# Attention's loads in another order on the load queue, with one-word stores between them that wait for computed tiles

## The chip, the cores and the metric

The kernel runs on one core of a Trainium2 chip. A core has a matrix engine (TensorE, PE in the profile; PEld are its weight loads), a vector engine (VectorE, DVE), a scalar engine (ScalarE, ACT), GpSimd (POOL) and SyncE (SP), which in this kernel issues every load and store. Each engine runs its own instructions in order and waits on semaphores for the others. Sixteen DMA engines move data between HBM and the core's memory. The metric is the device time of one execution in microseconds: 512.07 is the median of three runs before the change (509.72 to 512.94).

## The reference

Three layers in float32, one behind the other. First attention with 4 batches, 8 heads, 512 local and 32 global tokens of 64 features: local tokens attend to a window of 32 positions on either side and to the global tokens, global tokens attend to all. Then a gated MLP, then a soft mixture of experts.

```python
k_all = np.concatenate([k_g, k_l], axis=2)
v_all = np.concatenate([v_g, v_l], axis=2)
out_g = np.matmul(sm(scale * np.matmul(q_g, k_all.transpose(0, 1, 3, 2))), v_all)
s_ll = scale * np.matmul(q_l, k_l.transpose(0, 1, 3, 2))
s_ll = np.where(np.abs(pos[:, None] - pos[None, :]) <= 32, s_ll, -1000000000.0)
s_lg = scale * np.matmul(q_l, k_g.transpose(0, 1, 3, 2))
out_l = np.matmul(sm(np.concatenate([s_lg, s_ll], axis=-1)), v_all)
...
x = (silu(x @ w_gate) * (x @ w_val)) @ w_out      # 2304 tokens, 512 -> 1536 -> 512
...
logits = x @ phi                                  # then 8 experts with 4 slots each
```

## The kernel before

Attention comes first and takes about the first 110 us of the span. It is cut into 8 steps n, each a batch with half of its heads, and each step into two halves tp; the 16 halves are the units u = 2n + tp. For every unit TensorE computes scores (`stage_scores`, L346), VectorE adds the mask and finds the largest (L357), ScalarE takes exponentials (`stage_exp`, L367), TensorE transposes them (`stage_pT`, L376), ScalarE copies the transposes into two tiles pT (L379), and TensorE multiplies them with the values (`stage_pv`, L390). This is a software pipeline: in the loop's pass u stand the scores and exponentials of unit u, the transposes and values of unit u - 1 and the last transposes (`stage_xT`) of unit u - 2. The global tokens of step n have their scores in its even unit (`stage_gscores`, L451; exponentials into pG, L466 to L473), and their values in the next step's even unit (`stage_gpv`, L499).

The loads of a step are queries qT (512 KB, `load_q`, L204), keys kS (736 KB, `load_k`, L208) and values (960 KB in five loads, `load_v`, L228 to L236). Each has two buffers by turns, so that a load of step n + 2 (for values: n + 1) waits until the work of the step that held the buffer has read it. GpSimd copies values into two shifted layouts (`turn_v`, L242 to L247) and spreads queries into the form that the scores need (`spread_q`, L264). A load waits also for the one that stands eight places ahead of it in the order of issue, since eight semaphores go around.

MLP's matrices come as 64-bit words that a helper turns into float32 in five steps p0 to p4 (`w_prep`): `w_load` brings a tile raw of 512 KB; p0 takes its absolute values on ScalarE (L136) and shifts on VectorE (L137); p2 issues the load of the tile two further on. In attention one such step runs in each unit (`prep_some`), right behind the unit's scores and ahead of the copies into pT. Steps are there from the end of unit 4 on, so that p0 of raw0 stands in unit 5 and p0 of raw1 in unit 10.

All loads stand in one queue of SyncE, in the order of the code. An instruction there that waits holds up all behind it. In the loop before, the calls stand in this order:

```python
load_k(n + 2)            # odd units, behind the exponentials
...
load_q(n + 2); load_v(n + 1)      # even units, at the end
...
if u == 2: w_load(0); w_load(1); # and phi
```

Of the kernel before, what the change touches and what calls it, by code (L numbers as in the profile page):

```python
# [8 lines left out]
F32 = mybir.dt.float32  # L9
# [11 lines left out]
P = 128  # L21
# [4 lines left out]
NQ = B * 2  # L26
# [10 lines left out]
def window(i):  # L37

    if i == 0:
        return 0, "A", 0  # L40
    m, k = divmod(i - 1, 3)
    return (4 * m, 4 * m + 2, 4 * m + 3)[k], "ABC"[k], m
# [3 lines left out]
def attention_moe_soft_moe_kernel(  # L46
# [15 lines left out]
    nc = tc.nc  # L62
# [19 lines left out]
    dram = ctx.enter_context(tc.tile_pool(name="dram", bufs=1, space=bass.MemoryType.DRAM))  # L82
# [6 lines left out]
    phi_sb = cpool.tile([P, NC, NS], F32, name="phi_sb")  # L89
# [4 lines left out]
    for i, (_, n) in enumerate(BLOCKS):  # L94
        pool = x2pool if i in GROUPS[-1] else x1pool
        t = pool.tile([P, 2 * NC * n * P], F32R, name=f"x{i}")
        t = t.rearrange("p (a c n) -> p a c n", a=2, c=NC)
# [9 lines left out]
    def ring_tile(i, name, dt=F32R):  # L107
        p = rings[0] if i % 3 == 0 else rings[1]
        return p.tile([P, 4, DM], dt, name=name, tag=f"w{i % 3}")

    def w_load(q):
        if q >= 3 * NFC:
            return
        c, k = divmod(q, 3)
        fs = slice(c * P, c * P + P)
        t = wraws[q] = wtmp.tile([P, NC * P, 2], U32, tag="raw", name=f"raw{q}", bufs=2)
        if k < 2:
            nc.sync.dma_start(
                t.rearrange("p (c f) w -> p c (f w)", c=NC),
                (w_gate, w_val)[k][:, fs].rearrange("(c p) f -> p c f", p=P).bitcast(U32),  # L120
            )
        else:
            nc.sync.dma_start(t.rearrange("p f w -> p (f w)"), w_out[fs, :].bitcast(U32))
# [3 lines left out]
    def w_prep(q):  # L127

        c, k = divmod(q, 3)
        d = {}  # L130

        def p0():
            raw = d["raw"] = wraws.pop(q)
            d["t"] = wtmp.tile([P, NC * P], U32, tag="wbits", name=f"wb{q}", bufs=3)
            d["v"] = wtmp.tile([P, NC * P], F32, tag="wabs", name=f"wv{q}")
            nc.scalar.activation(d["v"], raw[:, :, 1].bitcast(F32), AF.Abs)  # L136
            nc.vector.tensor_scalar(  # L137
                out=d["t"], in0=raw[:, :, 1], scalar1=3, scalar2=0x3FFFFFFF,
                op0=ALU.logical_shift_left, op1=ALU.bitwise_and,
            )  # L140

        def p1():
            nc.vector.scalar_tensor_tensor(  # L143
                out=d["t"], in0=d["raw"][:, :, 0], scalar=29, in1=d["t"],
                op0=ALU.logical_shift_right, op1=ALU.bitwise_or,
            )

        def p2():
            nc.vector.scalar_tensor_tensor(  # L149
                out=d["t"], in0=d["raw"][:, :, 1], scalar=0xC0000000, in1=d["t"],  # L150
                op0=ALU.bitwise_and, op1=ALU.bitwise_or,
            )
            w_load(q + 2)

        def p3():
            w = d["t"].bitcast(F32)
            nc.vector.scalar_tensor_tensor(  # L157
                out=w, in0=d["v"], scalar=F64_NORMAL, in1=w, op0=ALU.is_ge, op1=ALU.mult
            )
            if k == 0:  # L160
                wchunk[c] = ring_tile(c, f"w{c}")
                wkept[c] = dram.tile([P, 4, DM], F32, name=f"w_d{c}")

        def p4():
            w = d["t"].bitcast(F32)
            if k == 2:
                wo[c] = w
                nc.sync.dma_start(wo_d[:, c], w)
                return
            wh, wl = wchunk[c][:, 2 * k], wchunk[c][:, 2 * k + 1]  # L170
            nc.scalar.activation(wh, w, AF.Copy)  # L171
            nc.gpsimd.tensor_tensor(out=wl, in0=w, in1=wh, op=ALU.subtract)  # L172
            ks = slice(2 * k, 2 * k + 2)
            nc.sync.dma_start(wkept[c][:, ks], wchunk[c][:, ks].bitcast(F32))

        prep.extend((p0, p1, p2, p3, p4))

    def prep_some(n=1):
        for _ in range(min(n, len(prep))):
            prep.pop(0)()  # L180
# [21 lines left out]
    def load_q(n):  # L202
        qT[n] = aqk.tile([P, 2, S], F32, tag="qT", name=f"qT{n}")
        nc.sync.dma_start(qT[n], qT_d[n])  # L204

    def load_k(n):
        kS[n] = aqk.tile([P, 2, KBLK * 32], F32, tag="kS", name=f"kS{n}")
        nc.sync.dma_start(kS[n], kS_d[n])  # L208
# [45 lines left out]
    def spread_q(n, a, eng, xs=slice(0, 16)):  # L254

        rows = slice(64 * a, 64 * a + 64)
        dst = qB[n % 2][rows].rearrange("p (a x g) -> p a x g", a=2, g=64)[
            :, :, xs, 32 * a : 32 * a + 32
        ]
        src = qT[n][rows].rearrange("p a (x q) -> p a x q", q=32)[:, :, xs]  # L260
        if eng is nc.scalar:
            nc.scalar.activation(dst, src, AF.Copy)
        else:
            eng.tensor_copy(dst, src)  # L264
# [28 lines left out]
    for g in (0, 1, 3, 2):  # L293
# [7 lines left out]
        for r in range(3):  # L301
            first = next(i for i in range(1, 16) if i % 3 == r and i % 2 == bl)
            p0 = first // 2
            n = len(range(p0, 8, 3))
            k = window(first)[1]
# [24 lines left out]
    st = {}  # L330
# [32 lines left out]
    def stage_exp(u):  # L363
        d = st[u]
        for hp in range(2):
            for bp in range(4):
                nc.scalar.activation(  # L367
                    d["p"][hp][:, bp], d["sm"][hp][:, bp], AF.Exp,
                    bias=d["nm"][:, hp, bp : bp + 1], scale=-1.0, accum_out=d["rs"][:, bp, hp : hp + 1],
                )  # L370

    def stage_pT(u, hp):
        d = st[u]
        pt = ps_tr.tile([P, 4, P], F32, tag="tr", name=f"ppT{u}_{hp}")
        for bp in range(4):
            nc.tensor.transpose(pt[:, bp], d["p"][hp][:, bp], ident)  # L376
        pT = awk.tile([P, 4, P], F32, tag=f"pT{hp}", name=f"pT{u}_{hp}")
        d["pT", hp] = pT
        nc.scalar.activation(pT, pt, AF.Copy)  # L379
# [34 lines left out]
    def split_rest():  # L414
        while rest:
            rest.pop(0)()
# [99 lines left out]

    mstack = ExitStack()
    NU = len(units)
    load_k(1)
    for u in range(NU):  # L520
        n, tp = units[u]
        stage_scores(u)
        split_rest()
        prep_some()
        if u >= 1:
            stage_pT(u - 1, 0)
            stage_pT(u - 1, 1)
        stage_exp(u)
        if tp == 1 and n + 2 < NQ:
            load_k(n + 2)  # L530
        if u == 0:

            turn_v(0, 0, 3)
        if tp == 0 and n + 1 < NQ:
            spread_q(n + 1, 0, nc.gpsimd)
        if u == 0:
            turn_v(0, 3, 5)
        if tp == 0 and n + 1 < NQ:
            if n > 0:
                spread_q(n + 1, 1, nc.gpsimd)  # L540
        if u == 1:
            spread_q(1, 1, nc.vector)
        if tp == 0:
            stage_gscores(n)
            stage_gexp(n)
        else:
            stage_gpT(n, 0)
        if u >= 1:
            stage_pv(u - 1)
        if tp == 1:  # L550
            stage_gpT(n, 3)
        if u >= 1 and tp == 0:
            stage_gpv(n - 1)
        if tp == 1 and n + 1 < NQ:
            turn_v(n + 1)
        if u >= 2:
            stage_xT(u - 2)
        if tp == 0 and n + 2 < NQ:
            load_q(n + 2)
        if tp == 0 and n + 1 < NQ:  # L560
            load_v(n + 1)
        if u == 2:
            w_load(0)
            w_load(1)
            nc.sync.dma_start(phi_sb, phi.rearrange("(c p) s -> p c s", p=P))
        if u == 4:
            for q in range(3):
                w_prep(q)
    for a in range(4):
        rows = slice(32 * a, 32 * a + 32)  # L570
        nc.gpsimd.tensor_copy(istack[rows], ident[rows, rows])
# [236 lines left out]
    gate(0, 0, G1[0], False)  # L808
    stage_pT(NU - 1, 0)
    stage_pT(NU - 1, 1)  # L810
    stage_xT(NU - 2)
    stage_gpv(NQ - 1)
    split_rest()
    stage_pv(NU - 1)
    prep_some(len(prep))
    gate(0, 0, G1[1], False)
    stage_xT(NU - 1)
    split_rest()
# [36 lines left out]
    for c in range(NFC):  # L855
# [6 lines left out]
        k = S1 * c + 13 if last else S1 * (c + 1) + 3  # L862
# [61 lines left out]
    t = epool[0].tile([P, 4096], F32, name="dr0", tag="e0")  # L924
    t = [t[:, 512 * k : 512 * k + 512] for k in range(5)]
# [17 lines left out]
    k = base + 30  # L943
# [148 lines left out]
    t = dpool.tile([P, 4 * NF], F32, tag="Ts", name="sT")  # L1092
    nc.gpsimd.memset(t[:, : 5 * E * DG], 0.0)  # L1093
    t = t[:, : 5 * E * DG].rearrange("p (c k) -> p c k", c=5)
# [69 lines left out]
    for k in range(3, 2 * E):  # L1164
# [4 lines left out]
        if side == 0:  # L1169
            t = epool[slot > 0].tile([P, 4096], F32, name=f"f{slot}", tag=f"e{slot}")  # L1170
# [22 lines left out]
    for i in range(5, NEARLY):  # L1193
        t = epool[1].tile([P, 4096], F32, name=f"ob{i}", tag=f"e{i}")
# [141 lines left out]
```

## Time and profile before

| | before |
|---|---|
| median of the runs | 512.07 us (509.72 to 512.94) |
| the profiled execution | 514.79 us, span 513.0 us |
| TensorE busy | 482.3 us, 94% |
| VectorE, ScalarE, GpSimd busy | 306.9, 181.4, 127.9 us |
| bytes moved by DMA | 107.63 MB |

The span runs from the first instruction of the program to its last in the profiled execution; starts below are counted from its beginning. TensorE's busy share is high everywhere but in the first twentieth. [...] A piece called issue in the chain of waits is time in which an engine waited for nothing that the profile shows.

### The profile page before, as it was taken

To read this page: it belongs to the slowest core of one execution; us is meant where nothing else is said; L and a number is where in the kernel's file an instruction comes from. 1 tells how busy PE (TensorE), PEld (TensorE's weight loads), DVE (VectorE), ACT (ScalarE), POOL (GpSimd) and SP (SyncE) were. 2 spreads that over 40 slices of the span, in tenths; PEclk is the share of its full clock that TensorE was granted. 3 is DMA by queue.
4 is the path that set the end of the run, shared out by engine and by line. 5 is a ranking of instruction groups with operands and counts; after the bars stand their busy time and mean duration, and the time that the engine had idled before them with its cause. 6 is when DMAs were issued, how large, how long until landed. Compare 5 with 4: busy or idle time off the path is not lost.

```text
span 513.0 us, 12537 instructions
## 1 busy us (share of the span) xinstructions
PE 482.3 (94%) x5092; PEld 379.7 (74%) x5092; DVE 306.9 (60%) x801; ACT 181.4 (35%) x542; POOL 127.9 (25%) x199
## 2 busy tenths in 40 slices
PE   6698999999999999999999999999999999889972
PEld 4587788788778788778777877787799988532741
DVE  7667888777976786777776677353233434452022
ACT  5868898892233222222223321121111012310021
POOL 7886798630322222112112221000000000010000
PEclk8999999999999999999999999999999999999997
DMA  8987585412744554444445473133099996699996
GB/s 216 298 224 230 172 262 148 120 44 63 227 167 149 166 181 145 161 160 165 143 145 169 152 248 135 56 118 132 6 380 391 411 414 212 241 423 419 357 349 193
DMA packets 50433, 107.63 MB, mean 210 GB/s; under 512 B 3464, under 2 KB 35016, under 8 KB 47176
## 3 DMA queue, kind: packets, MB, share of 16 engines
q1 hardware_dynamic: 50376, 106.84, 61.5%
q8 instruction: 40, 0.66, 0.5%
q14 instruction: 17, 0.14, 0.1%
HBM read 86.64 MB, written 20.19 MB: 208 GB/s over the span
## 4 chain that ended last, share of the span: by engine, by line
PE 80%; ACT 5%; DVE 5%; DMA 5%; issue 2%; SPq 2%; ACTq 0%; DVEq 0%
PE pval L602 28%; PE pgate L602 28%; PE sc L346 4%; PE psh L1132 3%; PE T L768 3%; PE o L390 2%; ACT p L367 2%; DMA f<-in_w_dram 2%; PE ppT L376 2%; DMA wo<-wo_d 2%; PE L L677 2%; SPq L900 2%; PE pwp L648 2%; DVE sm L357 1%; PE pwt L638 1%
## 5 line engine op out<-in xcount | busy, mean ns | idle before, releaser
L602 PE MATMUL pgate<-x,w 128*128 128x512 f32 x432 | 108.8, 396 | 0.0
L602 PE MATMUL pval<-x,w 128*128 128x512 f32 x432 | 107.1, 396 | 0.0
L602 PEld LDWEIGHTS pval<-x,w 128*128 128x128 f32 x432 | 80.2, 188 | 20.0 <-issue 2.2
L602 PEld LDWEIGHTS pgate<-x,w 128*128 128x128 f32 x432 | 80.2, 188 | 17.6
L617 DVE SCALAR_TENSOR_TENSOR u<-u,pgate 128x512 f32<-128x512 f32 (+2 forms) x60 | 36.5, 608 | 77.4 <-ACT u L616 76.2
L616 ACT ACTIVATE u<-pgate 128x512 f32<-128x512 f32 (+2 forms) x60 | 31.8, 530 | 126.9 <-PE pgate L602 68.3
L172 POOL TENSOR_TENSOR w<-wb,w 128x512 fp32r<-128x512 f32 x24 | 31.4, 1308 | 110.6 <-ACT w L171 62.6
L626 DVE SCALAR_TENSOR_TENSOR u<-u,pval 128x512 f32<-128x512 f32 (+2 forms) x60 | 36.3, 605 | 35.7 <-PE pval L602 35.7
L367 ACT ACTIVATE p<-sm,nm 128x128 f32<-128x128 f32 x128 | 49.4, 393 | 0.0
L602 PE MATMUL pval<-x,wr 128*128 128x384 f32 (+1 forms) x288 | 47.8, 312 | 0.0
L171 ACT ACTIVATE w<-wb 128x512 fp32r<-128x512 f32 x24 | 15.2, 632 | 92.1 <-DVE wb L157 49.4
L602 PE MATMUL pgate<-x,wr 128*128 128x384 f32 (+1 forms) x288 | 47.7, 311 | 0.0
L602 PEld LDWEIGHTS pval<-x,wr 128*128 128x128 f32 x288 | 43.3, 188 | 5.1 <-issue 5.1
L602 PEld LDWEIGHTS pgate<-x,wr 128*128 128x128 f32 x288 | 43.5, 188 | 3.8 <-issue 3.7
L346 PE MATMUL sc<-kS,qB 128*64 128x128 f32 x512 | 34.2, 282 | 6.0 <-ACT pG L470 3.0
L346 PEld LDWEIGHTS sc<-kS,qB 128*64 128x64 f32 x512 | 28.7, 139 | 11.1 <-issue 6.2
L357 DVE CUSTOM_DVE_ANT_0 sm<-sc,masks 128x128 f32<-128x128 f32 x128 | 28.6, 287 | 6.4 <-PE sc L346 4.6
L1093 POOL MEMSET sT<- 128x1440 f32 x1 | 1.3, 1297 | 123.7 <-PE U L1068 123.7
L157 DVE SCALAR_TENSOR_TENSOR wb<-wv,wb 128x512 f32<-128x512 f32 x36 | 24.9, 692 | 3.8 <-DVE wb L149 0.5
L660 POOL COPY wp<-ws 32x32 f32<-32x32 f32 x48 | 11.8, 246 | 60.2 <-DVE ws L653 58.7
L629 DVE STREAM_TRANSPOSE hT<-u 128x512 f32<-128x512 f32 x36 | 25.6, 712 | 1.3
L143 DVE SCALAR_TENSOR_TENSOR wb<-raw,wb 128x512 uint32<-128x512 uint32 x36 | 25.0, 693 | 1.1
(209 smaller groups left out, 728.6 us busy)
## 6 DMA issues: line engine op xcount, KB each, us to landing
e<-in_w_dram SPq DMA_DIRECT2D x7, 2048.0 KB, 13.1
w_d<-w SPq DMA_DIRECT2D x24, 512.0 KB, 2.6
wr<-w_d SPq DMA_DIRECT2D x12, 1024.0 KB, 7.1
f<-in_w_dram SPq DMA_DIRECT2D x10, 1024.0 KB, 12.8
raw<-in_wgate_dram SPq DMA_DIRECT2D x12, 512.0 KB, 3.6
raw<-in_wval_dram SPq DMA_DIRECT2D x12, 512.0 KB, 4.0
raw<-in_wout_dram SPq DMA_DIRECT2D x12, 512.0 KB, 3.6
kS<-in_kS_dram SPq DMA_DIRECT2D x7, 736.0 KB, 7.0
```

Source lines behind the costliest of these rows:

```text
L143: nc.vector.scalar_tensor_tensor(out=d["t"], in0=d["raw"][:, :, 0], scalar=29, in1=d["t"], op0=ALU.logical_shift_right, op1=ALU.bitwise_or,)
L157: nc.vector.scalar_tensor_tensor(out=w, in0=d["v"], scalar=F64_NORMAL, in1=w, op0=ALU.is_ge, op1=ALU.mult)
L172: nc.gpsimd.tensor_tensor(out=wl, in0=w, in1=wh, op=ALU.subtract)
L346: nc.tensor.matmul(sc[64 * (i % 2) : 64 * (i % 2) + 64, i // 2], qb[:, hp, blk], kS[n][:, hp, 32 * s0 : 32 * s0 + 128], start=True, stop=T ...
L357: nc.vector.tensor_tensor_reduce(out=sm[:, bp], in0=sc[:, bp], in1=masks[:, 4 * tp + bp], scale=-SCALE, scalar=3e38, op0=ALU.add, op1=ALU.min,
L367: nc.scalar.activation(d["p"][hp][:, bp], d["sm"][hp][:, bp], AF.Exp, bias=d["nm"][:, hp, bp : bp + 1], scale=-1.0, accum_out=d["rs"][:, b ...
L602: nc.tensor.matmul(ps[:, :n], w[:, 2 * k + a, cc * P : cc * P + P], xt[b][:, cc], start=(cc == 0 and i == 0), stop=(cc == NC - 1 and i == 2),)
L616: nc.scalar.activation(u[:, :n], pg[:, :n], AF.Tanh, scale=0.5)
L617: nc.vector.scalar_tensor_tensor(out=u[:, :n], in0=u[:, :n], scalar=1.0, in1=pg[:, :n], op0=ALU.add, op1=ALU.mult)
L626: nc.vector.scalar_tensor_tensor(out=u[:, :n], in0=u[:, :n], scalar=0.5, in1=pv[:, :n], op0=ALU.mult, op1=ALU.mult)
L629: nc.vector.transpose(out=hT[blk][:, c], in_=u[:, :n])
L768: nc.tensor.matmul(d["T"][i][32 * gg : 32 * gg + 32, 0:NF], rs[bi][r, 32 * j : 32 * j + 32], hT[blks[bi]][r, :, 32 * j : 32 * j + 32], sta ...
```

## The change

Only calls that issue loads are put elsewhere, and five stores are added. `pace(k, t)` stores one element of a tile t into a small DRAM tile; its place in SyncE's queue makes the queue wait until t is computed. Keys and queries of step 2 stand in unit 1 behind such a store of pT of unit 0, so that the values of step 1 are ahead of them. Queries of step 3 stand in unit 3. Queries of step n + 2 for n from 2 to 5 stand early in unit 2n, behind a store of pT of unit 2n - 1. The loads raw0, raw1 and phi move from unit 2 to units 4, 6 and 7. What the steps of `w_prep` do, and where, is as before.

```diff
--- before.py
+++ after.py
@@ -516,6 +516,12 @@
 
     mstack = ExitStack()
     NU = len(units)
+    paced = dram.tile([1, 16], F32, name="paced")
+
+    def pace(k, t):
+
+        nc.sync.dma_start(paced[:, k : k + 1], t)
+
     load_k(1)
     for u in range(NU):
         n, tp = units[u]
@@ -525,8 +531,17 @@
         if u >= 1:
             stage_pT(u - 1, 0)
             stage_pT(u - 1, 1)
+        if u == 1:
+            pace(0, st[0]["pT", 0][0:1, 0, 0:1])
+            load_k(2)
+            load_q(2)
+        if tp == 0 and n > 1 and n + 2 < NQ:
+            pace(n, st[u - 1]["pT", 0][0:1, 0, 0:1])
+            load_q(n + 2)
         stage_exp(u)
-        if tp == 1 and n + 2 < NQ:
+        if tp == 1 and 0 < n and n + 2 < NQ:
+            if n == 1:
+                load_q(3)
             load_k(n + 2)
         if u == 0:
 
@@ -535,9 +550,8 @@
             spread_q(n + 1, 0, nc.gpsimd)
         if u == 0:
             turn_v(0, 3, 5)
-        if tp == 0 and n + 1 < NQ:
-            if n > 0:
-                spread_q(n + 1, 1, nc.gpsimd)
+        if tp == 0 and n + 1 < NQ and n > 0:
+            spread_q(n + 1, 1, nc.gpsimd)
         if u == 1:
             spread_q(1, 1, nc.vector)
         if tp == 0:
@@ -555,17 +569,16 @@
             turn_v(n + 1)
         if u >= 2:
             stage_xT(u - 2)
-        if tp == 0 and n + 2 < NQ:
-            load_q(n + 2)
         if tp == 0 and n + 1 < NQ:
             load_v(n + 1)
-        if u == 2:
+        if u == 4:
             w_load(0)
-            w_load(1)
-            nc.sync.dma_start(phi_sb, phi.rearrange("(c p) s -> p c s", p=P))
-        if u == 4:
             for q in range(3):
                 w_prep(q)
+        if u == 6:
+            w_load(1)
+        if u == 7:
+            nc.sync.dma_start(phi_sb, phi.rearrange("(c p) s -> p c s", p=P))
     for a in range(4):
         rows = slice(32 * a, 32 * a + 32)
         nc.gpsimd.tensor_copy(istack[rows], ident[rows, rows])
```

The first place is SyncE's queue in units 0 to 2 (vA, vB, vC are the values' layouts, the number behind a name is the step or the buffer). Before:

```order
L208 DMA kS1_198<-in_kS_dram 128x1472
L204 DMA qT2_267<-in_qT_dram 128x1024
L228 DMA vA1_117<-in_vl_dram 96x5x256
L229 DMA vA1_117<-in_vg_dram 32x5x256
L233 DMA vB1_118<-in_vl_dram 32x256
L235 DMA vC1_119<-in_vl_dram 64x4x256
L236 DMA vC1_119<-in_vl_dram 32x256
L208 DMA kS2_328<-in_kS_dram 128x1472
L204 DMA qT3_535<-in_qT_dram 128x1024
```

And with the change:

```order
L208 DMA kS1_199<-in_kS_dram 128x1472
L228 DMA vA1_117<-in_vl_dram 96x5x256
L229 DMA vA1_117<-in_vg_dram 32x5x256
L233 DMA vB1_118<-in_vl_dram 32x256
L235 DMA vC1_119<-in_vl_dram 64x4x256
L236 DMA vC1_119<-in_vl_dram 32x256
L523 DMA paced_198<-pT0_0_310 1x1
L208 DMA kS2_320<-in_kS_dram 128x1472
L204 DMA qT2_322<-in_qT_dram 128x1024
```

The five loads of the second values moved up two places past the third queries, and a store stands between them and the third keys.

The second place is the same queue in units 2 to 4, from the last load of the third values on. Before:

```order
L236 DMA vC0_116<-in_vl_dram 32x256
L118 DMA raw0_542<-in_wgate_dram 128x4x256
L118 DMA raw1_544<-in_wval_dram 128x4x256
L565 DMA phi_sb_81<-in_phi_dram 128x4x32
L208 DMA kS3_602<-in_kS_dram 128x1472
L204 DMA qT4_815<-in_qT_dram 128x1024
L228 DMA vA1_117<-in_vl_dram 96x5x256
```

With the change, from the queries of step 3 on:

```order
L204 DMA qT3_597<-in_qT_dram 128x1024
L208 DMA kS3_599<-in_kS_dram 128x1472
L523 DMA paced_198<-pT3_0_699 1x1
L204 DMA qT4_709<-in_qT_dram 128x1024
L228 DMA vA1_117<-in_vl_dram 96x5x256
L229 DMA vA1_117<-in_vg_dram 32x5x256
L233 DMA vB1_118<-in_vl_dram 32x256
L235 DMA vC1_119<-in_vl_dram 64x4x256
L236 DMA vC1_119<-in_vl_dram 32x256
L118 DMA raw0_820<-in_wgate_dram 128x4x256
L208 DMA kS4_881<-in_kS_dram 128x1472
```

raw0 stood right behind the third values; it now stands behind the five loads of the fourth values, and raw1 and phi are further back. The keys of step 3 are no longer behind them.

The third place is ScalarE in units 4 and 5 with the change, with the semaphores that each instruction waits for; the rows are the same before but for numbers.

```order
L473 ACTIVATE pG_112,grs2_733<-gt2_722,gm2_729 128x32 [waits PE_49,Activation_49]
L409 ACTIVATE x0_82<-pxT2_809 128x2x256 [waits PE_49]
L136 ACTIVATE wv0_856<-raw0_820 128x512 [waits DMAHW3_49]
L379 ACTIVATE pT4_0_864<-ppT4_0_859 128x512 [waits PE_49,Activation_49]
L379 ACTIVATE pT4_1_871<-ppT4_1_866 128x512 [waits PE_49,Activation_49]
L367 ACTIVATE p5_0_822,rs5_824<-sm5_0_826,nm5_825 128x128 [waits DVE_49,Activation_49]
```

Nothing moved on ScalarE: the first work on raw0 stands ahead of the copies into pT4 and the exponentials p5. The orders of TensorE, VectorE and GpSimd are the same as well.

## Rows read from the trace of the kernel before

**Rows 1.** The page's part 1: engine, busy us, share of the span, instructions.
```profile
PE 482.3 (94%) x5092; PEld 379.7 (74%) x5092; DVE 306.9 (60%) x801; ACT 181.4 (35%) x542; POOL 127.9 (25%) x199
```

**Rows 2.** Chain of waits in order of time, first 160 us: start, us, what.
```profile
18.17 1.90 PE sc L346 x32
...
22.49 2.81 issue
...
28.89 1.90 PE sc L346 x32
...
34.18 1.90 PE sc L346 x32
...
39.89 1.75 issue
...
60.15 1.90 PE sc L346 x32
...
84.79 1.90 PE sc L346 x32
```

**Rows 3.** DMA view, queue 8: 22.7 to 22.8, 26.7 to 26.9, 39.1 to 39.3.
```profile
q8 instruction: 1, 0.02, 77.6%
...
q8 instruction: 1, 0.02, 30.0%
...
q8 instruction: 1, 0.02, 34.3%
```

**Rows 4.** DMA view, 16.0 to 22.7: queue, kind: packets, MB, share of 16 engines.
```profile
q1 hardware_dynamic: 1206, 1.72, 110.5%
q14 instruction: 1, 0.01, 0.5%
```

**Rows 5.** Sums by stretch: stretch, us, busy us (instructions), granted clock, DMA share, GB/s.
```profile
25.30:28.20 2.90, 2.90 (x105) 2.83 (x105) 0.99 (x4) 0.71 (x6) 2.72 (x3) 0.52 0.15 58
38.00:39.90 1.90, 1.89 (x115) 1.74 (x112) 1.64 (x5) 1.90 (x11) 1.78 (x3) 1.00 0.99 389
39.90:41.60 1.70, 0.00 (x0) 0.00 (x0) 1.21 (x5) 1.70 (x10) 0.97 (x1) 1.00 0.37 98
```

**Rows 6.** Timeline of SyncE: start, us, engine line op out<-in, count.
```profile
11.97 0.33 SPq L204 DMA_DIRECT2D qT<-in_qT_dram  x1
...
15.68 0.37 SPq L208 DMA_DIRECT2D kS<-in_kS_dram  x1
...
28.24 0.34 SPq L228 DMA_DIRECT2D vA<-in_vl_dram  x1
...
30.95 0.42 SPq L118 DMA_DIRECT2D raw<-in_wgate_dram  x1
...
39.91 0.34 SPq L228 DMA_DIRECT2D vA<-in_vl_dram  x1
```

**Rows 7.** Timeline of ScalarE; in brackets idle time before, and what ended it.
```profile
15.82 1.09 ACT L379 ACTIVATE pT<-ppT 128x512 f32<-128x512 f32 x2 [1.50 <-PE ppT L376]
...
25.37 0.28 ACT L470 ACTIVATE pG<-gs,gm 128x32 f32<-128x32 f32 x1
...
43.07 0.68 ACT L136 ACTIVATE wv<-raw 128x512 f32<-128x512 f32 x1
45.12 1.09 ACT L379 ACTIVATE pT<-ppT 128x512 f32<-128x512 f32 x2 [1.37 <-PE ppT L376]
```

**Rows 8.** Tile raw, first 100 us: issue to landing, over its four loads.
```profile
DMA to landing us min/median/max: 3.6/3.6/7.6
```

**Rows 9.** Timeline of GpSimd.
```profile
21.89 1.25 POOL L242 COPY vB<-vA 64x1280 f32<-64x1280 f32 x1 [1.52 <-DMA vA<-in_vl_dram]
...
28.20 2.12 POOL L264 COPY qB<-qT 64x1024 f32<-64x1024 f32 x2
```

**Rows 10.** Tile vA, first 100 us: issue to landing.
```profile
DMA to landing us min/median/max: 3.9/5.4/9.9
```

## The prediction

> **What bounds the kernel now.** I read the page's busy shares first, then the chain of waits in order of time, then the timelines of the engines around the places that the change touches. TensorE is busy for 94% of the span [rows 1], and all that the change moves is loaded before 100 us, so the question is how evenly the sixteen units of attention follow each other. In the chain, the scores of unit 2 start at 18.17, of unit 4 at 34.18, of unit 8 at 60.15 and of unit 12 at 84.79 [rows 2]. From 60.15 to 84.79 two units take 24.64 / 2 = 12.3 us, which is the steady pace. From unit 2 to unit 4 they take 16.0, from unit 4 to unit 8 13.0 per two units. So before unit 8 the pipeline loses 3.7 + 1.3 = 5.0 us. That sum caps what any better loading can give, unless the steady pace itself changes: 512.07 - 5.0 = 507.1.
>
> Where the 5.0 us lie: the chain holds two pieces called issue, 2.81 us at 22.49 and 1.75 us at 39.89 [rows 2]. In both TensorE stops in the middle of a run of matmuls on tiles that it has just used, so no tile is late. The DMA view says what is: a single packet of 0.02 MB on queue 8, whose kind is "instruction", is served just after 22.7 and another just after 39.1 [rows 3]. TensorE goes on at 25.30 and 41.64, about 2.5 us behind each packet. In the 6.7 us ahead of the first, queue 8 served nothing while 1.72 MB of loads passed on queue 1 [rows 4]. I read this as TensorE running dry because the fetch of its next instructions stands behind attention's loads. [...]
>
> **The change part by part.**
>
> *A, the first gap.* Before, third queries are issued at 11.97, then second values, and third keys at 15.68 [rows 6]. After, the values take the place at 11.97, and third keys and queries come behind a store that waits for the first transposed tile, pT0. ScalarE copies both halves of it from 15.82 on in 1.09 us [rows 7], so the first is there at about 16.4; with the store's issue the keys move from 15.68 to about 17. Thus 512 KB = 0.52 MB are out of the way of the fetch, at 1.72 MB in 6.7 us, 0.257 MB per us [rows 4], and it is served 2.0 us earlier. If the keys also come into the queue behind the fetch, it is earlier still, and the whole 2.81 goes. If the fetch does not stand behind loads, nothing goes. I take -2.0, bounds -2.8 and 0. With 0.8 us of gap left, shorter than the 1.75 that left the clock alone, the slow stretch goes too. At clock 0.52, 105 matmuls took 2.90 us; at 1.00, 115 took 1.89 [rows 5]. 105 x 1.89 / 115 = 1.73, so -1.2, bounds -1.2 and 0. ScalarE allows this: the second half of unit 3's scores needs the read of pG that starts at 25.37 and takes 0.28 [rows 7], while the scores that start at 28.89 [rows 2] would start 3.2 us earlier, at 25.7, and reach their second half later. Nothing can give more than the 3.7 us of this stretch.
>
> *B, the next fetch.* It is served just after 26.7 now [rows 3], long after the last load was issued. After, 736 + 512 KB = 1.28 MB of keys and queries follow the values; at 0.257 MB per us they pass for 5.0 us from about 20.7, up to 25.7, just when TensorE, now 3 us ahead, wants this fetch. It could be hidden (0) or come about 2 us late. I take +0.5.
>
> *C, the first weights.* Before, raw0 is issued at 30.95, and ScalarE's first work on it (L136, unit 5) starts at 43.07 with no wait [rows 7]. After, raw0 is issued in unit 4 behind the five loads of v3, whose first waits until TensorE has read those values' buffer (39.91 now [rows 6]). Behind v2's first load raw0 came 30.95 - 28.24 = 2.71 us later [rows 6], so it is issued at 39.91 + 2.71 = 42.62 on the old clock, and 43.07 is when it must have landed. The loads of raw tiles land 3.6 us after issue where nothing is ahead, and up to 7.6 behind v2 and another raw tile [rows 8]. So ScalarE waits until between 46.2 and 50.2. ScalarE works in order, and behind L136 stand the copies of pT4, the exponentials of unit 5 and, through them, TensorE's value matmuls of units 4 and 5. The copies of pT4 start at 45.12 now, after 1.37 us of idling [rows 7] that covers a part. L136 takes 0.68, so they start between 46.9 and 50.9: +1.8 to +5.8. Between the ends: here v3's 960 KB are ahead and no second raw tile, so I take the landing at 5.2 us, and 42.62 + 5.2 + 0.68 = 48.5, which is +3.4. The gap at 39.89 costs nothing more, since raw0's time counts from reads that end before it.
>
> *D, the clock again.* From the end of unit 4's transposes until pT4 is there TensorE has nothing to do for some 3 us, as long as the gap at 22.49. I charge the same slow stretch, +1.2, bounds 0 and 1.7 (a stretch 1.4 times as long).
>
> *E, what is nearly free.* The paced stores take an issue slot of SP's each, about 0.35 us like its other issues [rows 6], and SP is on no path there. What stands behind them (queries two steps ahead, and values that wait for a later read by TensorE anyway) has time. The copies of the second values on GpSimd start at 21.89 after 1.52 us of waiting for their load, those of the third queries at 28.20 [rows 9]; earlier values let GpSimd start near 20.5 and need the queries by 26.7, about when they land. From unit 6 on, queries come some 3 us later than now, just ahead of the values; a load of values landed in 3.9 to 9.9 us after issue [rows 10], and GpSimd's copies of them are wanted only two units on. 0, at worst +0.5. The second raw tile and phi are used far later than their new places.
>
> **The sum.** -2.0 - 1.2 + 0.5 + 3.4 + 1.2 = +1.9 us. The profiled execution took 514.79 (span 513.0 and 1.8 around it), 2.7 above the median of 512.07; it becomes 516.7, and the median 514.0. The good ends of A to D, -3.7 + 0 + 1.8 + 0, give -1.9, or 510.2; the gain of A halved and C at its end, -1.6 + 0.5 + 5.8 + 1.7, give +6.4, or 518.5.
>
> [...]
>
> **The rivals.**
>
> *The weights come early enough.* If raw0 lands 3.6 us after issue, TensorE's pause is 1.6 us shorter and may leave the clock alone, as the gap at 39.89 did; with A at its cap and B hidden that is the good end above, 510.2. It goes below this only if raw0 lands faster than any row shows; I allow 508.5. For it: no second raw tile and no phi load compete. Against: 960 KB of values are issued right ahead of raw0, while nothing stood ahead of the raw tiles that took 3.6.
>
> *The gap stays and the weights are late.* If the gap at 22.49 has another cause than the loads, or only moves to the next fetch, A is 0 and the rest stays: 3.4 + 1.2 + 0.5 = +5.1, or 517.2; with raw0 landing 6.2 us after issue it is 518.2. It is slower by over 1% from the point where raw0 needs more than 5.2 us and TensorE still stands at 22.49. For it: no late tile proves the cause of the gap. Against: packet and end of gap go together twice.
>
> *The change moves nothing that can be measured.* If the order of issue mattered neither for the fetch nor for raw0 (landing inside ScalarE's idle time), the time stays at 512. Against: L136 would have to find a tile 0.45 us after its issue. It lies inside the forecast's range and has no chance of its own beyond 2 in 100.
>
> **How the numbers follow.** My forecast, a gain in units 2 to 4 that the wait for raw0 takes back (511 to 516.5, centre 514.0): 0.62. First rival (508.5 to 511): 0.18. Second (516.5 to 520): 0.18. The range that leaves out no more than 2 in 10 is 508.5 to 518.5. About 1%, 5.1 us, is what a measurement of this kernel can tell from no change. Faster by over 1% means below 507.0, the cap itself, beyond the first rival's far end: 0.06 for what I have not seen. Slower by over 1% means above 517.2, most of the second rival: 0.13. Within 1%: the rest, 0.81.
>
> **What would show it.** A: the issue piece near 22.5 is 0 to 1 us long, queue 8's packet there comes near 20.7, the scores of unit 4 start near 31, and the stretch behind has clock 1.00. B: any issue piece near 26. C: ScalarE's L136 waits for the DMA of raw0 for about 5 us near 40 to 45, the largest wait of ScalarE in attention. D: a granted clock near 0.5 behind it. From unit 8 on the pace is 12.3 us per two units as now. I am wrong if L136 does not wait, if the gap at 22.5 is as long as before, or if the steady pace changes.

## The result, and the profile after

The changed kernel takes 517.5 us (median of 14 runs, 515.72 to 519.49) beside 514.25 for the kernel before on the same chip: a ratio of 1.0078, with a 95% interval of 1.0057 to 1.0098. On the median of 512.07 that is 516.1, or +4.0 us where +1.9 was forecast; it is slower, but by less than the 1% named in the prediction. The profiled execution took 518.45 us, span 516.7.

The page's first lines, with the same columns as [rows 1]: TensorE is as busy as before.

```profile
span 516.7 us, 12552 instructions
## 1 busy us (share of the span) xinstructions
PE 484.0 (94%) x5092; PEld 380.9 (74%) x5092; DVE 307.9 (60%) x801; ACT 181.0 (35%) x542; POOL 127.6 (25%) x199
```

The chain of waits of the changed kernel in order of time (start, us, what), to be read against [rows 2]:

```profile
19.89 1.97 PE sc L346 x32
...
24.29 0.70 issue
...
32.81 2.02 PE sc L346 x32
...
41.35 5.61 DMA raw<-in_wgate_dram
...
47.55 0.59 ACT pT L379
48.19 1.93 PE o L390 x64
50.12 0.83 PE pg L483 x3
50.95 0.85 PE pxT L425 x4
51.81 2.87 PE sc L346 x32
...
64.93 1.90 PE sc L346 x32
```

The stop at 22.49 has shrunk from 2.81 to 0.70 us (now at 24.29), and the stop of 1.75 us at 39.89 is gone. In their stead the chain runs through a load, that of raw0, for 5.61 us, and behind it the same kinds of matmul take up to twice as long: 1.93 us for 64 value matmuls that take 1.03 to 1.15 in the profile before at a clock of 1.00, 2.87 for 32 score matmuls that take 1.90 there. Counted from one unit's first score to another's, units 2 to 4 took 16.0 us before and 12.9 after, units 4 to 6 13.7 and 19.0, units 6 to 8 12.3 and 13.1, and from unit 8 to unit 12 the pace is that of before. Unit 2 itself starts 1.8 us later, which the section on the prediction comes back to. Units 12 to 14 took 13.1 us where it was 12.1, so that unit 14 starts 5.7 us late; from there to the end the changed profile takes 414.1 us and that of before 416.1, and the spans differ by 3.7. What made these last two differences was not tried.

Where the wait is: the timeline of ScalarE and that of SyncE in the changed kernel (start, us, engine, line, operation, out<-in, count; in brackets idle time before, and what ended it), against [rows 6, 7].

```profile
46.98 0.66 ACT L136 ACTIVATE wv<-raw 128x512 f32<-128x512 f32 x1 [5.71 <-DMA raw<-in_wgate_dram]
47.55 1.06 ACT L379 ACTIVATE pT<-ppT 128x512 f32<-128x512 f32 x2
```

```profile
38.67 0.34 SPq L228 DMA_DIRECT2D vA<-in_vl_dram  x1
...
41.35 1.30 SPq L118 DMA_DIRECT2D raw<-in_wgate_dram  x1
```

raw0 is issued 2.68 us behind the first load of the values and lands 5.6 us after that, which is within the 3.6 to 7.6 of [rows 8]. ScalarE does nothing else in these 5.71 us: the copies into pT4 stand behind L136, and start at 47.55. TensorE pays for it, and then pays in clock; sums by stretch, columns as in [rows 5]: stretch, us, busy us of PE, PEld, DVE, ACT and POOL, granted clock of TensorE as a share of full speed, DMA share, GB/s.

```profile
24.90:27.80 2.90, 2.82 (x121) 2.56 (x123) 2.59 (x8) 2.90 (x17) 2.78 (x3) 1.00 0.23 86
...
48.20:53.80 5.60, 5.60 (x91) 5.10 (x93) 2.62 (x5) 4.33 (x19) 3.21 (x3) 0.50 0.01 3
```

Behind the first, short stop the clock stays at 1.00, where it was 0.52 before. Behind the wait for raw0 it is 0.50 up to 53.8, about 6.8 us in all, twice as long as the 3.4 us behind the gap at 22.49.

### The profile page after: what moved, and what is told of

It reads as the page before. It is cut to its first block, busy times and chain, and to the rows that moved or that the text cites. A ratio compares the mean times of both kernels' runs of the same rounds, so it can differ in the third digit from the quotient of the medians.

```text
span 516.7 us, 12552 instructions
## 1 busy us (share of the span) xinstructions
PE 484.0 (94%) x5092; PEld 380.9 (74%) x5092; DVE 307.9 (60%) x801; ACT 181.0 (35%) x542; POOL 127.6 (25%) x199
## 4 chain that ended last, share of the span: by engine, by line
PE 80%; DMA 5%; ACT 5%; DVE 3%; SPq 3%; POOL 1%; issue 1%; ACTq 0%; DVEq 0%
PE pval L615 28%; PE pgate L615 28%; PE sc L346 3%; PE T L781 3%; PE psh L1145 3%; DMA f<-in_w_dram 2%; PE o L390 2%; PE L L690 2%; PE ppT L376 2%; ACT p L367 2%; SPq L913 2%; DMA vA<-in_vl_dram 2%; PE pwp L661 2%; DMA raw<-in_wgate_dram 1%; PE pwt L651 1%
## 5 line engine op out<-in xcount | busy, mean ns | idle before, releaser
L629 ACT ACTIVATE u<-pgate 128x512 f32<-128x512 f32 (+2 forms) x60 | 31.8, 530 | 127.0 <-PE pgate L615 68.3
L615 PE MATMUL pgate<-x,wr 128*128 128x384 f32 (+1 forms) x288 | 47.7, 312 | 0.0
L346 PE MATMUL sc<-kS,qB 128*64 128x128 f32 x512 | 35.7, 289 | 6.4 <-ACT pG L470 3.6
L346 PEld LDWEIGHTS sc<-kS,qB 128*64 128x64 f32 x512 | 30.1, 145 | 12.2 <-ACT pG L470 5.3
L136 ACT ACTIVATE wv<-raw 128x512 f32<-128x512 f32 x36 | 24.0, 665 | 7.5 <-DMA raw<-in_wgate_dram 7.5
```

Of the source, the lines that this page charges most:

```text
L346: nc.tensor.matmul(sc[64 * (i % 2) : 64 * (i % 2) + 64, i // 2], qb[:, hp, blk], kS[n][:, hp, 32 * s0 : 32 * s0 + 128], start=True, stop=T ...
L615: nc.tensor.matmul(ps[:, :n], w[:, 2 * k + a, cc * P : cc * P + P], xt[b][:, cc], start=(cc == 0 and i == 0), stop=(cc == NC - 1 and i == 2),)
L629: nc.scalar.activation(u[:, :n], pg[:, :n], AF.Tanh, scale=0.5)
```

## The experiments

All ratios are to the kernel before on the same chip, with 95% intervals. "Old order" means that queries and keys of step 2 stand as before; "store" is the one-word store of `pace`.

### Halves of the change

**The weights alone** (the kernel before, with raw0, raw1 and phi where the change has them):

```diff
-        if u == 2:
-            w_load(0)
-            w_load(1)
-            nc.sync.dma_start(phi_sb, ...)
         if u == 4:
+            w_load(0)
             for q in range(3):
                 w_prep(q)
+        if u == 6:
+            w_load(1)
+        if u == 7:
+            nc.sync.dma_start(phi_sb, ...)
```

> The kernel before, with only the weights' part of the change (raw0 in unit 4, raw1 in unit 6, phi in unit 7). Theory (the wait of L136 for raw0 costs about 5 us): unit 4 starts 16.0 us behind unit 2 as before, L136 waits 4 to 6 us, unit 6 starts about 19 us behind unit 4 (13.7 before), ratio to before 1.011 (1.008 to 1.013). Rival (the loss comes from the order of the attention loads): no change, 0.998 to 1.002.

Measured: 1.0098 (1.0073 to 1.0123), +5.0 us. The chain of waits of this kernel shows the wait again:

```profile
23.14 1.16 issue
...
32.95 1.90 PE sc L346 x32
...
42.00 4.98 DMA raw<-in_wgate_dram
...
51.83 3.02 PE sc L346 x32
```

Units 4 to 6 take 18.9 us, L136 waits for 5.71 us, and the clock is low from 47.3 to 54.1 (0.50 from 48.2 to 53.8). So the late weights cost what they cost with or without the new order. Two more things are to be seen: all loads up to 23 us are those of the kernel before, and yet the first stop is 1.16 us long, not 2.81, and the clock stays at 1.00 behind it.

**The order alone** (the changed kernel, with raw0, raw1 and phi back in unit 2: the diff above, reversed):

> The changed kernel with raw0, raw1 and phi back in unit 2. Theory: the gap of 2.8 us near 22.5 shrinks to under 1 us as in the changed kernel, unit 4 starts 12.5 to 13 us behind unit 2, L136 does not wait, ratio to before 0.994 (0.991 to 0.998), as three microseconds are won and nothing is given back. Rival: the order itself loses, ratio 1.004 to 1.008.

Measured: 0.9978 (0.9956 to 0.9999), -1.1 us: at the edge of the range that I expected, and the gain is less than half of its centre. The timeline of TensorE of this kernel says where it went:

```profile
23.93 0.24 PE L390 MATMUL o<-vC,pT 128*32 128x64 f32 x1 [0.39 <-issue]
...
40.02 0.32 PE L499 MATMUL og<-vC,pGT 128*32 128x64 f32 x7 [2.04 <-issue]
```

The first stop is all but gone, and unit 4 starts at 32.2, 1.9 us earlier than before. Then the other stop, 1.75 us before, is 2.04 here, with a clock of 0.51 from 41.5 to 45.0 behind it, and unit 6 starts at 47.7 as it did before.

**The kernel before, profiled once more** (no edit):

> The kernel before, profiled a second time. Theory (the first gap depends on how far the fetch of instructions is behind the loads, which varies from execution to execution): a gap of 0.7 to 2.8 us between 22 and 25.5, and unit 4 12.8 to 16 us behind unit 2; the average is then less than the 2.8 that the first profile showed. Rival: 2.6 to 3.0 us as before.

Measured: 514.7 us, span 512.9. The timeline of TensorE:

```profile
26.00 0.24 PE L390 MATMUL o<-vC,pT 128*32 128x64 f32 x1 [1.45 <-issue]
...
41.60 0.32 PE L499 MATMUL og<-vC,pGT 128*32 128x64 f32 x7 [1.53 <-issue]
```

The same code, and the first stop is 1.45 us and not 2.81, with the clock at 1.00 behind it. Unit 2 starts at 20.16 here and at 18.10 in the first profile; unit 4 at 34.29 and 34.11. What the first profile was early in unit 2 it lost in the stop.

### Where the weights may stand

**raw0 in unit 3** (the changed kernel, raw0 ahead of the fourth values instead of behind them):

```diff
+        if u == 3:
+            w_load(0)
         if u == 4:
-            w_load(0)
             for q in range(3):
```

> The changed kernel with the load of raw0 alone moved from unit 4 to the end of unit 3, behind the third step's queries and keys, where the queue idles. Theory: raw0 is issued near 30.3 and lands before 38, L136 does not wait, unit 6 starts 12.5 to 14 us behind unit 4 instead of 19.0, ratio to before 0.993 (0.990 to 0.997). Rival: as the changed kernel, 1.006 to 1.010.

Measured: 0.9927 (0.9908 to 0.9946), 510.21 us. It beats both kernels. raw0 is issued at 29.64 and lands 9.0 us later, at 38.7. Timelines of ScalarE and TensorE:

```profile
40.53 0.69 ACT L136 ACTIVATE wv<-raw 128x512 f32<-128x512 f32 x1
```

```profile
32.24 1.97 PE L346 MATMUL sc<-kS,qB 128*64 128x128 f32 x32
...
44.82 1.97 PE L346 MATMUL sc<-kS,qB 128*64 128x128 f32 x32
```

L136 starts without idle time ahead of it, units 4 to 6 take 12.6 us, and no stop of TensorE for which the profile shows no cause is above 0.7 us in attention. From the changed kernel to this one, by one load moved, is 1.0078 - 0.9927 = 0.0151, or 7.7 us.

**The work on raw0 one unit later** (the changed kernel, `w_prep` from unit 5 on, so that L136 stands in unit 6):

```diff
         if u == 4:
             w_load(0)
+        if u == 5:
             for q in range(3):
                 w_prep(q)
```

> The changed kernel with all loads where they are, but the preparation steps of the weights one unit later, so that L136 on raw0 stands in unit 6. Theory (the wait costs, not the load's traffic): L136 waits under 1 us, unit 6 starts 12.5 to 14 us behind unit 4, ratio to before 0.994 (0.991 to 0.998). Rival (raw0's traffic behind the fourth values costs): unit 6 stays 17 us or more behind unit 4, ratio 1.005 or more.

Measured: 1.0019 (0.9998 to 1.0039). The mechanism held: L136 does not wait, and units 4 to 6 take 12.1 us. The time did not follow. This one profile shows a reason: the later steps of `w_prep` move too. The third raw tile, issued by one of them, now falls together with the loads of unit 8, and eight loads are issued in 5 us. SyncE's timeline and TensorE's:

```profile
61.59 0.33 SPq L123 DMA_DIRECT2D raw<-in_wout_dram  x1
62.02 0.25 SPq L523 DMA_DIRECT2D paced<-pT  x1
62.36 0.33 SPq L204 DMA_DIRECT2D qT<-in_qT_dram  x1
62.87 0.34 SPq L228 DMA_DIRECT2D vA<-in_vl_dram  x1
...
66.45 0.35 SPq L208 DMA_DIRECT2D kS<-in_kS_dram  x1
```

```profile
75.79 0.27 PE L390 MATMUL o<-vC,pT 128*32 128x64 f32 x1 [2.16 <-issue]
```

TensorE stops for 2.16 us at 73.64, the clock is 0.50 from 75.7 to 79.1, and units 10 to 12 take 15.6 us instead of 12.4. The old stop came back in a new place, with a new bunch of loads ahead of it; no run takes that bunch away again.

### What the gain of raw0 in unit 3 is made of

Each of these is that version with a part taken back.

**Old order, weights spread, no store** (the kernel before with raw0 in unit 3, raw1 in 6, phi in 7):

> The kernel before with its order of attention's loads, and with raw0 in unit 3, raw1 in unit 6 and phi in unit 7. Theory (two separate gains: about 1 us by the order, 2 to 3 us by taking raw1 and phi out of unit 2): no wait of L136, the gap near 38 to 40 under 1 us, ratio 0.995 (0.993 to 0.997). Rival (only the two together gain): 0.998 to 1.002.

Measured: 0.9988 (0.9967 to 1.0008); first stop 1.54 us, the later one 0.43. Spreading the weights alone gives nothing that can be told from zero, as the rival had it.

**Without the first store** (only the line `pace(0, ...)` is taken out; keys of step 2 are then issued at 15.97 instead of 18.43):

> The kernel with raw0 in unit 3, without the first one-word store, so that the third keys and queries are issued right behind the second values. Theory (the keys then stand ahead of the first fetch): keys issued near 15.7 to 16.5, a first gap of 0.5 to 2 us, ratio to before 0.994 to 0.998. Rival (the store changes nothing, the third keys' place does not matter): 0.991 to 0.994 as with it.

Measured: 0.9945 (0.9924 to 0.9966), no stop near 24. Not to be told from the version with it.

**Without the later stores** (the block `pace(n, ...)`, `load_q(n + 2)` is taken out, and queries stand ahead of the values as before):

> The kernel with raw0 in unit 3, without the stores of units 4 to 10; the queries behind them go back to the end of the even units, ahead of the values, and are so issued 2 to 3 us earlier. Theory (the later stores cost and give nothing): pace of 12.1 to 12.6 us per two units from unit 4 on, ratio to before 0.993 (0.990 to 0.996), as with them. Rival (holding the queries back keeps fetches free): a gap of 1 to 2 us near 36 to 40 and ratio 0.996 to 1.000.

Measured: 0.9954 (0.9934 to 0.9974), no first stop, the later one 1.74 us. The ratio is still in the theory's range, the stop is the rival's.

**Without any store** (both edits):

> The kernel with raw0 in unit 3, with no store at all: only the second values ahead of third keys and queries, the order of the fourth queries, and the weights spread. Theory (what gains is the order and the spread weights): ratio 0.994 (0.991 to 0.997). Rival (the stores gain): 0.998 to 1.001.

Measured: 0.9985 (0.9960 to 1.0009), and both stops are there, in the timeline of TensorE:

```profile
25.57 0.24 PE L390 MATMUL o<-vC,pT 128*32 128x64 f32 x1 [2.49 <-issue]
...
40.89 0.32 PE L499 MATMUL og<-vC,pGT 128*32 128x64 f32 x7 [1.26 <-issue]
```

Its interval does not meet that of the version with both kinds of store. So the stores are worth about 0.0058, 3 us, and the new order without them nothing that can be told. Which kind of store gives how much is not told apart.

**Stores kept, queries of step 2 ahead of the values as before:**

```diff
             load_k(2)
-            load_q(2)
...
+        if u == 0:
+            load_q(2)
         if tp == 0 and n + 1 < NQ:
             load_v(n + 1)
```

> The kernel with raw0 in unit 3 and all stores, but with the third queries back ahead of the second values; third keys stay behind the first store. Theory (what gains are the stores and the spread weights, not the order of values and queries): first gap 0 to 1.5 us, ratio to before 0.994 (0.991 to 0.996). Rival (the values' place ahead of the queries gains): 0.996 to 1.000.

Measured: 0.9956 (0.9935 to 0.9976). The values' place ahead of the queries, which the change is named for, adds at most 0.003, inside the intervals. Its one stop in this stretch is 1.42 us at 26.09.

### The cause of the stops

**The two first raw tiles loaded in unit 0** (the kernel before, with both `w_load` calls moved ahead of the queries and values of unit 0, to put more loads ahead of the first fetch):

> The kernel before, with raw0 and raw1 (1.05 MB) loaded in unit 0 ahead of the third queries and second values instead of in unit 2; TensorE's work at the first gap uses nothing of what is behind them. Theory (the fetch of instructions stands behind loads that were issued before it): queue 8's first packet is served 3 to 4 us later, near 25 to 26.5, and the gap in the value matmuls of unit 1 is 4 to 7 us. Rival (the queues take turns, and the gap has another cause): first packet at 21 to 23, gap 1 to 3 us. Its time: 514 to 520.

Measured: 515.38 us (one time); the first packet of queue 8 is served at 22.5, no later than before, with a stop of 0.94, and the next stop is 2.29 us at 28.85. The theory missed, and the packet's time is the rival's; but the test was poor: the keys slipped from 15.68 to 18.82, and from 11.9 us to 17 us 2464 KB of loads were issued, hardly more than the 2208 KB of the kernel before. My reading is that the keys waited for raw0, which is issued eight places ahead of them: in the kernel before SyncE waited for 2.0 us with the queries of 11.97, until the load eight places ahead of them had landed. No row of this run shows it.

**A copy of 2 MB behind the values of unit 8** (raw0 in unit 3, and an extra transfer from DRAM to DRAM that nothing reads):

```diff
+        if u == 8:
+            nc.sync.dma_start(aside_d, w1[0])
```

> The kernel with raw0 in unit 3, with one more transfer of 2 MB from DRAM to DRAM that nothing reads, issued in unit 8 behind the sixth values, where TensorE has no gap now; the next values are not needed for 12 us. Theory (a fetch of instructions stands behind transfers that were issued before it): one fetch is served 4 to 8 us late, a gap of 2 to 6 us in TensorE between 66 and 80, and the time rises by 3 to 7 us over the kernel without the copy (510). Rival (the queues take turns, so that a fetch is hardly delayed): no gap over 0.6 us there, time 509 to 511.5.

Measured: 516.04 us (one time), beside 510.21 for the version without the copy. The timeline of TensorE, in a place where no kernel above had a stop:

```profile
81.99 0.43 PE L346 MATMUL sc<-kS,qB 128*64 128x128 f32 x2 [2.39 <-issue]
```

Queue 8's tenth and eleventh packet are served at 72.7 and 79.6, against 68.3 and 73.9 without the copy: 2.1 and 9.1 us behind unit 10's first score instead of 0.9 ahead of it and 4.65 behind. TensorE stops from 79.60 until 2.4 us behind the eleventh; units 10 to 12 take 16.6 us. With the copy two fetches thus came late, by 3.0 and 4.5 us against unit 10's first score, and such a stop with them. The copy went in 32 packets of 64 KB, of 2.5 to 3.8 us each (those of attention's loads have at most 5.9 KB). The tenth packet of queue 8 was served among the second sixteen (DMA view, 72.59 to 73.9):

```profile
q1 hardware_dynamic: 16, 1.05, 258.7%
q8 instruction: 1, 0.02, 5.6%
```

So it did not have to wait for all that was issued before it. The eleventh came behind the step's own queries and values. These values landed late as well, so it is not the cleanest of tests, and it is one profile.

**What the traces say together.** None of these edits touches the order of TensorE's instructions. The first stop begins 4.39 or 4.40 us behind the first score of unit 2 in all eight profiles that have one of 0.7 us or more at that place (before: 22.49 - 18.10; the second profile of it: 24.55 - 20.16; changed: 24.29 - 19.89). The later one begins 5.77 or 5.78 us behind the first score of unit 4 in seven profiles (39.89 - 34.11; 37.98 - 32.20 with the order alone). So TensorE stops at the same instruction each time, and only the end of the stop moves, 2.4 to 3.0 us behind the start of a packet of queue 8. I read that as a fetch of instructions that comes late, since the packet's kind is "instruction"; no tile has to do with it.

Counting TensorE's records bears that out (matmuls, weight loads and those of its queue). 449 of them stand ahead of the first stop and 1217, or 449 + 3 x 256, ahead of the later one. All 42 stops called issue of more than 0.35 us behind the first 15 us, in all fourteen profiles, stand behind 449 + 256 k records with a whole k, and each ends 2.2 to 3.1 us behind the start of queue 8's packet k, counted from 0. So each packet, of 16,384 bytes in the profiles before and after, goes with the next 256 of TensorE's instructions in this program. Where the first packet came 3.1 us or more before TensorE got to the first place, as in five profiles, there is no stop.

The same count shows that the packets come later under loads. Take, for each fetch in attention (the first 18 packets of a profile), the time from TensorE's start on the 256 instructions before to the packet. In the 54 fetches with queue 1's share of the engines, as in [rows 4], below 10% in the 3 us ahead of the packet it is 0.6 to 1.6 us, median 0.8, but for one served during the wait for raw0. In the 103 with a share of 90% or more it is 0.2 to 6.6 us, median 2.5. All stops of 0.7 us or more in attention have a share of 95% or more there.

How much was loaded sorts the later stop in the twelve profiles that have such a sum. The DMA view of the 6 us ahead of the packet (queue, kind: packets, MB, share of 16 engines) is this in the version without the later stores, where the stop is 1.74 us:

```profile
q1 hardware_dynamic: 919, 2.15, 103.0%
```

and this in the changed kernel, which has none there:

```profile
q1 hardware_dynamic: 645, 1.59, 87.1%
```

| MB on queue 1 in the 6 us ahead of the packet | stop, us |
|---|---|
| 2.07, 2.15, 2.16, 2.16, 2.21 (before, no later stores, before again, no stores, order alone) | 1.75, 1.74, 1.53, 1.26, 2.04 |
| 1.94, 1.88 (weights spread, raw0 in unit 3) | 0.43, 0.68 |
| 1.92, 1.84, 1.80 (no first store, queries first, work one unit later) | none |
| 1.59, 1.54 (changed, weights alone) | none |

The 6 us were chosen after the fact, and two profiles have no such sum: with the copy and with the raw tiles first, TensorE had stopped at an earlier instruction (34.48 and 28.85) and the fetches lie otherwise. Elsewhere the same sum does not sort the profiles. For the first stop 1.46, 1.43 and 1.24 MB go with 2.81, 1.45 and 2.49 us; ahead of the stops in units 10 and 11 it is 1.27 MB (2.16 us, work one unit later) and 1.35 (2.39 us, with the copy). Two kernels that are one and the same up to unit 4, without the first store and without any, had that fetch served at 19.8 and at 23.0, so a single profile says little of it. The means say more: in the seven profiles with the first store the first stop is 0 to 1.00 us long, mean 0.3, and in the seven without it 0 to 2.81, mean 1.5. With raw0 in unit 3 and no copy, the later stop is 0, 0 and 0.68 us with the later stores, and 0.43, 1.26 and 1.74 without them.

## Why the prediction was right, and where it was not

**Sign and size.** Within 1% and on the slow side, 516.1 in a range of 508.5 to 518.5. In steps, each the difference of two measured ratios: order alone -1.1 us; raw1, phi and raw0 spread over units 3 to 7 another -2.6 (0.9927 - 0.9978); raw0 in unit 4 and not 3 +7.7; together +4.0. Against their place in unit 2 the weights thus cost 5.1.

**A, the first gap.** The stop shrank to 0.70 us, where I had 0.8, the clock stayed up, and queue 8's packet came 2.45 us behind unit 2's first score instead of 4.63, so 2.2 us sooner where I had 2.0. From unit 2 to unit 4 the two profiles differ by 3.2 us, which is the very sum I had for A. That is luck, and A is still the step that failed. The price rested on one profile. Four profiles have the old order and the loads up to there as before: the stop is 2.81, 1.45, 1.16 and 1.54 us long in them, and only the first has a slow stretch behind it. Unit 4 starts at 34.1, 34.3, 32.9 and 34.2, mean 33.9. In the seven with the new order's keys behind the first store it starts at 30.9 to 32.7, mean 32.1. The gain up to unit 4 is about 1.8 us, not 3.2, and the order alone ends at -1.1 (the changed kernel against the weights alone: -1.0). A's own bounds, 0 to -4.0, held that; its value was the top of one execution. The reason was right in that the fetch came late behind loads [rows 4]. But I counted the 512 KB of queries moved out of its way, and in the version with these queries back ahead of the values and the stores kept the packet came 0.6 us behind unit 2's first score, with no first stop. So the store that holds the keys back helps, and the queries' move is not shown to.

**B, the next fetch.** I looked for it near 26, and no stop is there in the changed kernel. In seven other profiles that fetch stopped TensorE for 0.4 to 1.4 us, with the raw tiles first for 2.29. The longer stop was two fetches further on, near 38, when raw1 and phi stay in unit 2 (2.04 us with the order alone). I had said that the second raw tile and phi are used far later than their new places; that is so, but I priced what their move does to the queue at nothing, and it is part of the -2.6.

**C, the weights.** Right in place and nearly in size: raw0 landed 5.6 us after its issue (5.2 forecast), L136 waited 5.71 us, and the copies into pT4 started 14.8 us behind unit 4's first score instead of 11.0, +3.8 where I had +3.4.

**D, the clock.** Right in kind, too small: I expected a pause of some 3 us and 1.2 us of loss, at most 1.7. TensorE paused for 5.16 us and ran at 0.50 for about 6.8. Without the stop of 1.75 us it had got to the wait sooner, 10.3 us behind unit 4's first score instead of 11.7, and the pause that I forecast had left that out. The rest of what units 4 to 8 lost is 5.4 + 0.8 - 3.8 = 2.4 us; in it lies also VectorE, whose L137 waited 3.3 us for raw0. C and D together are 5.0 us by the weights alone and 5.1 by the changed kernel against the order alone (1.0078 - 0.9978); the forecast had 4.6. So of the miss of 2.1 us, 1.6 is A's and B's (1.1 us gained where I had 2.7) and 0.5 that of C and D.

**E.** SyncE's issues and the late queries cost nothing that shows; GpSimd's copies of the second values waited 1.06 us for their load, 1.52 before [rows 9]. The stores, which I had down as nearly free, are what gains: 3 us in the version with raw0 in unit 3.

**The rivals.** That the weights come early enough was wrong for this change, and right for the one with raw0 in unit 3, whose 0.9927 is 508.3 on the median of 512.07. That the gap stays and the weights are late named 517.2; the time came out between it and my forecast, since less than half of the gain of A and B was there to be had.

**The fetch and the loads.** That a fetch stands behind all loads issued before it was too strong a reading: the tenth packet in the run with the copy was served among the second sixteen of the copy's 32 packets, though the copy had been issued before, at 68.13. Yet under loads fetches came up to 6.6 us behind TensorE's start on the instructions before (0.8 is the median without loads), so A is not nothing. What a late fetch waits for no row shows, and that stays open.

**The start.** Unit 2's first score came at 18.0 to 20.4 in the fourteen profiles; the 1.8 us between before and after are inside this spread. In the five where it came at 20.0 or later, TensorE had waited 1.8 to 2.0 us at 8.7, and the clock was low in a stretch that ended at 18.4 to 19.3 (0.50 from 15.6 to 19.0 in the second profile of the kernel before). In the changed kernel's profile the chain up to there runs through the load of the first values, which the change does not touch and which needed 8.86 us from issue to landing (7.87 before):

```profile
4.00 8.86 DMA vA<-in_vl_dram
```

What sets this in one execution and not in the next was not tried.

## What to carry to other kernels

Before a stop is priced from a trace, profile the same code again: the kernel before stopped both times 4.39 us behind unit 2's first score, once for 2.81 us and once for 1.45. A load that is moved later must be held against the first instruction on its tile and what that engine has queued behind it: here one unit too late cost 7.7 us, and one unit earlier made the same change the best version. Transfers that nobody waits for can still go with late fetches of instructions: with the copy of 2 MB two of them came 3.0 and 4.5 us later, and TensorE stopped for 2.39 us. Spreading the weights alone gave nothing that can be told here; together with the new order and one-word stores of computed tiles in the load queue it gave 0.0073, 3.7 us.

## What the runs showed of the hardware

- TensorE stopped for up to 2.81 us with nothing in the profile that it waited for, in all 42 stops of more than 0.35 us behind 449 + 256 k of its records, and until 2.2 to 3.1 us behind the start of a packet of queue 8, whose kind is "instruction". At most fetches it did not stop: the profiles before and after have 40 such packets each, and 4 and 2 stops of more than 0.35 us behind the first 15 us. The stops of 0.7 us or more in attention all came behind 3 us of loads at a share of 95% or more.
- Behind pauses of TensorE of 5.16 and 5.17 us the clock was at 0.50 for 6.8 us. Behind stops of 2.04, 2.16, 2.29, 2.39 and 2.81 us it was low for 3.4 (0.50 to 0.52 in the sums of four of them); behind one of 2.49, and those of 1.75 and less, it stayed at 1.00.
- The same kernel, profiled twice, was 2.1 us apart at unit 2's start, 0.2 us at unit 4's and 0.1 us in its span (513.0 and 512.9).
